# Sending the last 7 MiB of zeros from SyncE's queue in a DMA-bound attention backward kernel

## The chip, the cores and the metric

The kernel runs on one core of one Trainium2 chip. The metric is the time of one execution in device microseconds. The kernel before takes 790.6 us, run after run within about 0.4 us (790.44 to 790.87 us).

Every profile below is of one execution. Its times start at the span's start, and the span ends with the last instruction. PE is TensorE, DVE is VectorE, ACT is ScalarE, POOL is GpSimd, SP is SyncE; a name with a q is that engine's own sequencer, which also issues DMAs.

## The reference, cut to what matters

One decoder block is run forward and backward. Attention reads only the last 4096 of 32768 cache positions, so the gradients of the two caches are zero in all other positions:

```python
W = min(4096, max(256, Sk // 4))           # 4096
k = jnp.repeat(k_cache[:, :, Sk - W:, :], rep, axis=1)
v = jnp.repeat(v_cache[:, :, Sk - W:, :], rep, axis=1)
...
_out, _vjp = jax.vjp(_f, A_x, A_k_cache, A_v_cache, A_wq, A_wo, B_w_gate, B_w_up, B_w_down)
```

The outputs out_2 and out_3 are the gradients of the K and V caches, each of shape (2, 8, 32768, 128) in bfloat16. They hold 224 MiB of zeros and 32 MiB of values. Weights, their gradients and the read part of the caches add some 60 MiB.

## The kernel before

The zeros come from a tile `zt` of 2048 bytes per partition. It is written to DRAM by a casting DMA (bytes in, float32 out), so one row of it makes 8192 bytes of zeros. GpSimd issues these DMAs. There are 32 zero regions of 7 MiB: 29 are issued early, three are cut into 15 pieces that go between the 16 late stores. Four of the early regions are cut unevenly over row counts such as 15 and 12, which gives the 16 DMA engines unequal shares.

```python
ZE = 2048
zt = const.tile([P, ZE], U8)
zero_regions = [o[b, g, 0:Z, :].rearrange("r d -> (r d)") for o in (out_2, out_3) for b in range(B) for g in range(HKV)]
ZPK = Z * DH // 2 // ZE                    # 896 packets of 8192 bytes in a region
ZERO_PARTS = {6: ((4, 1), (15, 2), (2, 2), (15, 14), (12, 2), (P, 4), (16, 7)), 12: ..., 18: ..., 24: ...}
ZERO_FIRST, ZERO_CUTS = 29, (1, 1, 1, 2, 2)
...                                        # zero_cast(i): one region; zero_next(): one late piece
x_bf = load_x(OFF_X)                       # SyncE's queue, 2 KB, the first load
wq_sb = at(OFF_WQ, [P, NDR, HQ * DH], BF16, "wq")
nc.sync.dma_start(out=wq_sb[:], in_=A_wq.rearrange("(p r) n -> p r n", r=NDR))
load_rows(nc.scalar)                       # two loads of 2 KB on ScalarE's queue
...
# the last part: 4 jobs x 2 groups x 2 stores of 2 MiB, from 8 buffers of 16 KB per partition
for a in range(2):
    g0 = gq * 4 + a * 2
    nc.gpsimd.dma_start(out=dst_v[:, b, g0:g0 + 2, :, :], in_=sts[a][:])
    zero_next()
```

The framework gives the DMAs of each issuing path eight completion semaphores (counters that a DMA raises when it has landed) in turn, so each GpSimd DMA waits for the landing of the eighth before it. At the end of the program SyncE waits for all semaphores in a fixed order and then all engines meet at a barrier, a point that none passes before all have reached it.

## Time and profile before

| | before |
|---|---|
| time, median of 4 runs | 790.57 us |
| span of the profiled execution | 788.88 us |
| DMA bytes | 332.44 MB |
| first packet of the first large load (wq) | 2.21 us |
| last DMA packet's end | 786.23 us |
| from that to the span's end | 2.65 us |

The last three rows are read from the trace's records of single DMA packets.

These lines are from the page of the kernel before. Each digit of the DMA line is the busy share of a fortieth of the span (19.7 us) in tenths, and the GB/s line gives what was moved in it. The q0 line is GpSimd's queue, the q1 line SyncE's.

```profile
span 788.9 us, 12410 instructions
...
DMA  8999999999999999999999999999999999999998
GB/s 366 419 417 422 420 426 426 421 430 428 427 422 420 424 425 422 425 425 430 427 428 429 426 430 426 422 430 425 428 428 428 423 429 427 427 428 427 427 429 320
...
q0 software_dynamic: 34576, 268.44, 88.7%
q1 hardware_dynamic: 6932, 63.19, 37.6%
```

The reader is to see a kernel bound by its DMA engines from beginning to end: only the first and last slice are slower. The table of windows of the kernel before says the same of the end. Its columns are the stretch, its length, the busy time of the five engines, TensorE's granted clock, the DMA share and GB/s.

```profile
700.00:740.00 40.00, 19.09 (x56) 6.35 (x57) 20.70 (x32) 16.78 (x29) 5.89 (x9) 0.71 1.07 427
740.00:760.00 20.00, 0.00 (x0) 0.00 (x0) 0.00 (x0) 0.00 (x0) 2.78 (x4) 0.50 1.06 428
```

After 740 us no engine computes, and DMA still moves 428 GB/s. What is left then is queued bytes.

The DMA view of the kernel before over the stretch 755 to 789 us, cut in 40 slices of 0.85 us, shows how the queue runs dry:

```profile
DMA  9999999999999999999999999999989786641000
GB/s 443 434 414 405 463 443 424 424 414 443 424 414 434 434 443 434 414 443 414 443 405 443 414 443 424 424 434 424 386 328 357 328 347 289 279 193 58 0 0 0
```

From about 778 us the rate falls in steps, because the 16 DMA engines do not end together. In the packet records three end about 7 us before the last one, two about 3 us, the rest within 2 us. Averaged over the 16 engines they stand idle for 2.2 us. The three zeros at the end of the line are time with no DMA at all.

Here is what SyncE waited for in the last 29 us of the kernel before (waits that end after 760 us). The columns are the sum, the number of waits and the longest of them.

```profile
SPq L870 <- DMA out_dram<-zt: 164.9, 1, 164.9
SPq L870 <- DMA out_dram<-mem: 14.4, 1, 14.4
SPq L870 <- PEq L870: 1.9, 2, 1.4
```

The middle line is the wait for the last store. The third line is the closing barrier: after everything had landed SyncE still waited 1.4 us for another engine. The profile names TensorE, but TensorE had been idle since before 740 us.

The first issues of SyncE and the first two steps of GpSimd's zeros (start, duration, engine, line, what, and the idle time before) in the kernel before:

```profile
0.81 0.36 SPq L141 DMA_DIRECT2D mem<-in_A_x_dram  x1
1.22 0.37 SPq L145 DMA_DIRECT2D mem<-in_A_wq_dram  x1
```

```profile
13.54 5.37 POOL L315 TENSOR_SCALAR zt<-mem 128x2048 uint8<-128x2048 uint8 x1 [9.84 <-DMA mem<-in_A_wq_dram]
19.22 6.93 POOL L114 DMA_DIRECT2D out_dram<-zt  x8 [0.31 <-POOL zt L315]
```

And GpSimd's last issues before the end:

```profile
745.54 0.71 POOL L844 DMA_DIRECT2D out_dram<-mem  x1 [4.43 <-DMA out_dram<-mem]
747.74 0.68 POOL L130 DMA_DIRECT2D out_dram<-zt  x1 [1.48 <-DMA out_dram<-zt]
752.88 0.71 POOL L844 DMA_DIRECT2D out_dram<-mem  x1 [4.46 <-DMA out_dram<-mem]
```

### The profile page before, as it was taken

To read this page: it belongs to the slowest core of one execution; us is meant where nothing else is said; L and a number is where in the kernel's file an instruction comes from. 1 tells how busy PE (TensorE), PEld (TensorE's weight loads), DVE (VectorE), ACT (ScalarE), POOL (GpSimd) and SP (SyncE) were. 2 spreads that over 40 slices of the span, in tenths; PEclk is the share of its full clock that TensorE was granted. 3 is DMA by queue.
4 is the path that set the end of the run, shared out by engine and by line. 5 is a ranking of instruction groups with operands and counts; after the bars stand their busy time and mean duration, and the time that the engine had idled before them with its cause. 6 is when DMAs were issued, how large, how long until landed. Compare 5 with 4: busy or idle time off the path is not lost. (4 is left out here: it accounts for less than half of the span.)

```text
span 788.9 us, 12410 instructions
## 1 busy us (share of the span) xinstructions
PE 560.2 (71%) x5032; PEld 301.8 (38%) x5096; DVE 474.1 (60%) x1161; ACT 280.7 (36%) x406; POOL 68.9 (9%) x103
## 2 busy tenths in 40 slices
PE   3899998787687989845558779787886675757000
PEld 3656564344565555423225544343332221212000
DVE  2699999126533989854612676755447998757000
ACT  1434330124345334102012426544443674656000
POOL 4300000002000000200000300000100111111100
PEclk9799999867699999987876869855685997788555
DMA  8999999999999999999999999999999999999998
GB/s 366 419 417 422 420 426 426 421 430 428 427 422 420 424 425 422 425 425 430 427 428 429 426 430 426 422 430 425 428 428 428 423 429 427 427 428 427 427 429 320
DMA packets 41578, 332.44 MB, mean 421 GB/s; under 512 B 2592, under 2 KB 2608, under 8 KB 2736
## 3 DMA queue, kind: packets, MB, share of 16 engines
q0 software_dynamic: 34576, 268.44, 88.7%
q1 hardware_dynamic: 6932, 63.19, 37.6%
q8 instruction: 40, 0.66, 0.3%
q10 hardware_dynamic: 12, 0.01, 0.1%
q14 instruction: 18, 0.15, 0.0%
HBM read 49.30 MB, written 282.33 MB: 420 GB/s over the span
## 5 line engine op out<-in xcount | busy, mean ns | idle before, releaser
L422 DVE TENSOR_TENSOR mem<-mem,ee 128x512 bf16<-128x512 bf16 x512 | 181.1, 419 | 26.6 <-PE KT_ps L378 17.4
L433 PE MATMUL M_ps<-mem 128*128 128x512 bf16 x468 | 136.3, 393 | 8.7 <-DVE mem L422 5.3
L836 PE MATMUL ps_g<-mem 128*128 128x512 bf16 x250 | 82.9, 437 | 40.5 <-DVE mem L91 37.7
L91 DVE CAST mem<-ps_g 128x512 bf16<-128x512 f32 x128 | 82.8, 687 | 26.4 <-DMA out_dram<-mem 15.3
L93 ACT CAST mem<-ps_g 128x512 bf16<-128x512 f32 x128 | 74.3, 585 | 50.9 <-PE ps_g L836 44.3
L380 ACT COPY mem<-KT_ps 128x1024 bf16<-128x1024 bf16 x64 | 63.0, 1014 | 69.4 <-PE KT_ps L378 65.5
L114 POOL DMA_DIRECT2D out_dram<-zt x52 | 40.3, 995 | 497.3 <-DMA out_dram<-zt 497.0
L836 PEld LDWEIGHTS <-mem 128*128 128x128 bf16 x256 | 27.5, 108 | 95.3 <-issue 84.3
L254 PE MATMUL ps_tb<-ident_bf,mem 128*128 128x128 bf16 x480 | 56.3, 251 | 9.4 <-DMA mem<-in_B_w_gate_dram 2.8
L433 PEld LDWEIGHTS <-mem 128*128 128x128 bf16 x512 | 43.8, 99 | 48.8 <-issue 15.4
L378 PE MATMUL KT_ps<-ident_bf,mem 128*128 128x128 bf16 x512 | 44.6, 229 | 20.1 <-DMA mem<-in_A_k_cache_dram 16.0
L93 ACT COPY mem<-ps_tb 128x512 bf16<-128x512 bf16 x44 | 25.7, 585 | 72.6 <-PE ps_tb L254 67.8
L254 PEld LDWEIGHTS <-mem 128*128 128x128 bf16 x480 | 37.5, 128 | 35.0 <-issue 30.8
L656 PE MATMUL VT_ps<-ident_bf,mem 128*128 128x128 bf16 x512 | 46.7, 239 | 3.2 <-ACT mem L93 1.1
L656 PEld LDWEIGHTS <-mem 128*128 128x128 bf16 x512 | 36.6, 107 | 27.7 <-issue 20.2
L91 DVE COPY mem<-ps_tb 128x512 bf16<-128x512 bf16 x44 | 18.7, 424 | 42.1 <-PE ps_tb L254 40.7
L665 PE MATMUL dP_ps<-mem 128*128 128x512 bf16 x114 | 40.4, 431 | 4.8 <-ACT mem L93 4.7
L378 PEld LDWEIGHTS <-mem 128*128 128x128 bf16 x512 | 33.6, 102 | 26.6 <-DMA mem<-in_A_k_cache_dram 16.6
L93 ACT COPY mem<-VT_ps 128x1024 bf16<-128x1024 bf16 x31 | 31.7, 1022 | 33.9 <-PE VT_ps L656 32.7
L727 PE MATMUL ps_gr<-mem 2*128 2x512 bf16 (+1 forms) x78 | 33.7, 497 | 12.8 <-DVE mem L747 7.4
L91 DVE CAST mem<-ps_gr 128x512 bf16<-128x512 f32 (+1 forms) x38 | 24.7, 655 | 27.8 <-PE ps_gr L727 27.8
L91 DVE COPY mem<-VT_ps 128x1024 bf16<-128x1024 bf16 x33 | 23.1, 700 | 27.9 <-PE VT_ps L656 27.5
(244 smaller groups left out, 627.1 us busy)
## 6 DMA issues: line engine op xcount, KB each, us to landing
out_dram<-zt POOLq DMA_DIRECT2D x25, 7168.0 KB, 85.5
out_dram<-mem POOLq DMA_DIRECT2D x16, 2048.0 KB, 33.7
mem<-in_A_k_cache_dram SPq DMA_DIRECT2D x16, 1024.0 KB, 21.0
mem<-in_A_v_cache_dram SPq DMA_DIRECT2D x16, 1024.0 KB, 22.0
out_dram<-zt POOLq DMA_DIRECT2D x4, 4096.0 KB, 57.7
out_dram<-zt POOLq DMA_DIRECT2D x6, 2048.0 KB, 32.8
out_dram<-zt POOLq DMA_DIRECT2D x9, 1024.0 KB, 34.0
out_dram<-mem SPq DMA_DIRECT2D x5, 1792.0 KB, 19.0
```

The costliest lines, as they stand in the source:

```text
L91: nc.vector.tensor_copy(out=out, in_=in_)
L93: nc.scalar.copy(out=out, in_=in_)
L114: nc.gpsimd.dma_start(out=dst[done * ZE:(done + rows * n) * ZE].rearrange("(p k e) -> p k e", p=rows, k=n), in_=src.unsqueeze(1).to_broadc ...
L254: nc.tensor.transpose(out=ps[:, a, :], in_=src_block(a), identity=ident_bf[:])
L378: nc.tensor.transpose(out=KT_ps[:, jj, :], in_=Kt[b, g][:, u * 8 + jj, :], identity=ident_bf[:])
L380: nc.scalar.copy(out=KT[:], in_=KT_ps[:])
L422: nc.vector.tensor_tensor(out=pk[:, :, i, :].rearrange("p j (d t) -> p j d t", t=2), in0=Kb[:, j0:j0 + pk_j, :].rearrange("p j (d t) -> p ...
L433: nc.tensor.matmul(out=M_ps[:], lhsT=Vt[b, g][:, j, :], rhs=pk[:, jj, :, :].rearrange("p i d -> p (i d)"), start=(j == 0), stop=(j == NJ - 1))
L656: nc.tensor.transpose(out=VT_ps[:, jj, :], in_=Vt[b, g][:, a * 8 + jj, :], identity=ident_bf[:])
L665: nc.tensor.matmul(out=dP_ps[:, c, :], lhsT=dOpad[:, w0:w0 + P], rhs=VT[:, c * 4:(c + 1) * 4, :].rearrange("d a k -> d (a k)"), start=(i = ...
L727: nc.tensor.matmul(out=ps[:, :n], lhsT=lhsT_fn(k), rhs=rhs_fn(k), start=True, stop=True)
L836: nc.tensor.matmul(out=ps[:, a2, :], lhsT=lhs_bf[:, jp * P:(jp + 1) * P], rhs=rhs_bd[:, ap * 2 + a2, gq * 4:(gq + 1) * 4, :].rearrange("q ...
```

## The change

The change is meant to shorten the end. The zeros are now counted in columns of 1 MiB. Of the 224 columns 205 instead of 203 go early, 12 go between the late stores, and the last 7 leave from SyncE's queue as a plain copy of a zeroed store buffer, with 14336-byte packets. That copy must wait until the last store but one has landed, because it uses its buffer. One column is cut so that eight copies on two rows ("pairs") with small packets stand among the first eight stores. Apart from this, the load of x moves from SyncE's queue to ScalarE's.

```diff
-    ZERO_FIRST, ZERO_CUTS = 29, (1, 1, 1, 2, 2)
...
+    ZCOLS, ZL = ZPK // P, 3584
+    z_cols, PAIR_COL = [0], 216
...
+    def zero_pair(n):
+        nc.gpsimd.dma_start(out=zero_dst(PAIR_COL * P + 112 + 2 * n, 2).rearrange("(p k e) -> p k e", p=2, k=2),
+                            in_=zt[0:P:P // 2, 0:ZE // 2].unsqueeze(1).to_broadcast([2, 2, ZE // 2]))
...
-    x_bf = load_x(OFF_X)
+    x_bf = load_x(OFF_X, nc.scalar)
...
-                for i in range(ZERO_FIRST):
-                    zero_cast(i)
+                zeros(205)
...
+        tail_zeros = list((1, 2, 1, 1, 1, 1, 1, 1, 0, 0, 0, 0, 0, 0, 3, 0))
...
                     nc.gpsimd.dma_start(out=dst_v[:, b, g0:g0 + 2, :, :], in_=sts[a][:])
-                    zero_next()
+                    zeros(tail_zeros.pop(0))
+                    if 0 <= n * 4 + gq * 2 + a < 8:
+                        zero_pair(n * 4 + gq * 2 + a - 0)
...
+        z_last = at(OFF_ST[(st_n[0] - 2) % len(OFF_ST)], [P, 2, ZL // 2], U32, "z_last")
+        nc.vector.memset(z_last[:, 0, :], 0)
+        nc.gpsimd.memset(z_last[:, 1, :], 0)
+        n_last = (len(zero_regions) * ZCOLS - z_cols[0]) * ZE // ZL
+        nc.sync.dma_start(out=zero_dst(z_cols[0] * P, n_last * P * ZL // ZE).bitcast(U32).rearrange("(p k e) -> p k e", p=P, k=n_last),
+                          in_=z_last[:].rearrange("p a e -> p (a e)").unsqueeze(1).to_broadcast([P, n_last, ZL]))
```

More of the change, by code (lines that the diff above doesn't have):

```diff
@@ L107 @@
     ZERO_PARTS = {6: ((4, 1), (15, 2), (2, 2), (15, 14), (12, 2), (P, 4), (16, 7)), 12: ((4, 1), (15, 2), (2, 2), (15, 14), (12, 2), (P, 4), (16, 7)), 18: ((4, 1), (15, 2), (2, 2), (15, 14), (12, 2), (P, 4), (16, 7)), 24: ((3, 16), (15, 2), (3, 4), (15, 18), (12, 2), (P, 4))}
-    ZERO_FIRST, ZERO_CUTS = 29, (1, 1, 1, 2, 2)
-    def zero_cast(i):
-        dst, done = zero_regions[i].bitcast(F32), 0
-        for rows, n in ZERO_PARTS.get(i, ((P, ZPK // P),)):
-            src = zt[0:rows * (P // rows):P // rows, :]
-            nc.gpsimd.dma_start(out=dst[done * ZE:(done + rows * n) * ZE].rearrange("(p k e) -> p k e", p=rows, k=n),
-                                in_=src.unsqueeze(1).to_broadcast([rows, n, ZE]))
-            done += rows * n
-        assert done == ZPK
@@ L119 @@
-    zero_pieces = []
-    for i in range(ZERO_FIRST, len(zero_regions)):
-        done = 0
-        for k in ZERO_CUTS:
-            zero_pieces.append(zero_regions[i].bitcast(F32)[done:done + P * k * ZE].rearrange("(p k e) -> p k e", p=P, k=k))
-            done += P * k * ZE
-        assert done == ZPK * ZE
-    def zero_next():
-        if zero_pieces:
-            dst = zero_pieces.pop(0)
-            nc.gpsimd.dma_start(out=dst, in_=zt[:].unsqueeze(1).to_broadcast([P, dst.shape[1], ZE]))
+    ZCOLS, ZL = ZPK // P, 3584
@@ new lines, with zero_dst, zero_rows @@
+    z_cols, PAIR_COL = [0], 216
+    def zero_dst(pk, n):
+        i, c = divmod(pk, ZPK)
+        assert c + n <= ZPK
+        return zero_regions[i].bitcast(F32)[c * ZE:(c + n) * ZE]
+    def zero_rows(pk, rows, n):
+        src = zt[0:rows * (P // rows):P // rows, :]
+        nc.gpsimd.dma_start(out=zero_dst(pk, rows * n).rearrange("(p k e) -> p k e", p=rows, k=n),
+                            in_=src.unsqueeze(1).to_broadcast([rows, n, ZE]))
+    def zero_pair(n):
+        nc.gpsimd.dma_start(out=zero_dst(PAIR_COL * P + 112 + 2 * n, 2).rearrange("(p k e) -> p k e", p=2, k=2),
+                            in_=zt[0:P:P // 2, 0:ZE // 2].unsqueeze(1).to_broadcast([2, 2, ZE // 2]))
@@ new lines, in zeros @@
+    def zeros(n):
+        while n:
+            i, c = divmod(z_cols[0], ZCOLS)
+            parts = ((16, 7),) if z_cols[0] == PAIR_COL else ZERO_PARTS[i] if c == 0 and n >= ZCOLS and i in ZERO_PARTS else ((P, min(n, ZCOLS - c, PAIR_COL - z_cols[0] if z_cols[0] < PAIR_COL else n)),)
+            done = 0
+            for rows, k in parts:
+                zero_rows(z_cols[0] * P + done, rows, k)
+                done += rows * k
+            z_cols[0] += -(-done // P)
+            n -= -(-done // P)
@@ L137, in load_rows, with load_x @@
         eng.dma_start(out=x_32, in_=A_x.rearrange("b s d -> (b s) d"))
-    def load_x(off):
+    def load_x(off, eng=nc.sync):
         x_bf = at(off, [B, D], BF16, "x")
-        nc.sync.dma_start(out=x_bf[:], in_=A_x.rearrange("b s d -> (b s) d"))
+        eng.dma_start(out=x_bf[:], in_=A_x.rearrange("b s d -> (b s) d"))
         return x_bf
-    x_bf = load_x(OFF_X)
+    x_bf = load_x(OFF_X, nc.scalar)
     wq_sb = at(OFF_WQ, [P, NDR, HQ * DH], BF16, "wq")
```

## The prediction

> **What bounds the kernel now.** The DMA engines. In the page's 40 slices the DMA row reads 9 in all but the first and last, and GB/s stays at 417 to 430 except there (366, 320). DMA moved 332.44 MB. TensorE is 71% busy, VectorE 60%, both idle after 740 us (table of windows). The chain of waits ends in stores. In the late packets an engine starts 8192 bytes every 0.305 us: 16 x 8192 / 0.305 us = 430 GB/s, which makes 774 us of all bytes (estimate), against 790.55. The gap: 2 us before the first load packet, ramp-up, 418 to 425 GB/s where loads and zeros mix, 2.3 us after the last landing, and the uneven end: three of 16 engines finish 6.8 to 7.4 us before the last, the others 0 to 3.7 us. The mean is 2.2 us (estimate), all that an even end could return.
>
> **What the change does.** Bytes stay: 224 MiB of zeros, 32 MiB of cache stores. (1) Two MiB more of zeros go early; the late 21 MiB on GpSimd's queue become 12 there and 7 on SyncE's. (2) Those 7 MiB are a plain copy of a zeroed store buffer, in 14336-byte packets. They wait for the landing of the last store but one and for two memsets, about 1.6 us (estimate, scaled from 0.27 us for 128x256); with issue some 3 us. Behind that store 5 MiB are queued, 12.2 us at 0.409 MiB/us. An engine 7 us ahead still has 2 us of work when SyncE's packets arrive: no gap. (3) Eight pair copies of 16 KB replace part of one column. GpSimd keeps at most eight DMAs outstanding (each waits for the eighth before it), so pairs cut its queue from 14 to 8 MiB, still 19 us of work. If each pair takes the next two engines, every engine keeps its bytes. (4) The load of x moves to ScalarE's queue: wq issues at 0.81 us instead of 1.22.
>
> The Trainium skill (DMA: Bandwidth & Descriptors, "Issuing engines are not separate DMA queues") says that all issuers' DMAs run on the same 16 engines and interleave. This trace agrees: 427 to 430 GB/s whether GpSimd writes alone (690 to 730 us) or SyncE's stores are mixed in (590 to 610). So the queue buys no bandwidth.
>
> **On the critical path.** (4): -0.4 us, since all transfers queue behind the first load. Larger packets (14336 bytes in 0.535 us at best, 8192 in 0.309): -0.1 us. SyncE's mix, 430 instead of 428 for 26 us: -0.1. More DMAs with completion writes: +0.1. A somewhat evener end: -0.5. Sum -1 us.
>
> **Predicted: 789.5 us, 787.6 to 790.7. Chances: faster by over 2% 0.01, within 2% 0.98, slower 0.01.**
>
> **What would show each step.** wq's issue at 0.8 us, the first zeros 0.4 us earlier. Of the last six slices only the last below 420 GB/s. SyncE's last DMA issued near 760 us, landing within 2.5 us of the span's end; the last store landing 5 to 15 us before it. Spread of the engines' last packets still 5 to 9 us. GpSimd's last store issued near 736 instead of 753.
>
> **What would make it wrong.** If the pairs all fall on few engines, or SyncE's packets lighten the late engines, the spread changes and up to 2 us are gained or lost. If compute paces stores 8 to 13, which have no zeros between them, DMA gaps appear near 700 to 735 us and it gets slower.

## The result

The changed kernel takes 789.36 us (median of 4 runs, 789.16 to 789.57) against 790.57 us (790.53 to 790.62). The ratio is 0.9985, with a 95% interval of 0.9967 to 1.0002: the same at the 2% limit, and 1.2 us less in the medians. (A ratio is the mean time of one kernel's fast runs over that of the other's fast runs of the same rounds, so it is not quite the ratio of the medians.) All four runs of the change are below all four of before, but the interval includes 1, so the size of the gain rests on the traces and on the runs below as well.

The page of the kernel after:

```profile
span 787.5 us, 12487 instructions
...
DMA  9999999999999999999999999999999999999998
GB/s 374 418 418 422 418 426 426 422 429 427 428 419 420 426 424 424 424 424 432 426 430 426 427 428 428 422 429 426 428 425 429 421 431 425 428 426 427 427 432 344
...
q0 software_dynamic: 33984, 261.10, 86.4%
q1 hardware_dynamic: 7456, 70.53, 40.5%
```

The 7 MiB have moved from q0 to q1, and the rates of the 38 middle slices are the same to within 3 GB/s. The windows of the kernel after have no gap in the DMA either, although no zeros stand between stores 8 and 13:

```profile
700.00:740.00 40.00, 22.65 (x68) 7.32 (x66) 23.20 (x36) 20.16 (x35) 8.81 (x13) 0.82 1.04 427
740.00:760.00 20.00, 0.00 (x0) 0.00 (x0) 1.55 (x1) 0.00 (x0) 1.60 (x1) 0.50 1.04 428
```

The DMA view of the kernel after over the same stretch, 755 to 789 us:

```profile
DMA  9999999999999999999999999999887877620000
GB/s 405 424 453 443 453 357 453 458 434 400 426 451 484 412 429 422 446 436 410 434 424 439 422 439 439 422 439 388 371 354 337 354 304 320 270 118 0 0 0 0
```

The staircase of the ending engines is the same as before, one slice earlier. The SyncE waits that end after 770 us, for the kernel after:

```profile
SPq L882 <- DMA out_dram<-mem: 26.1, 2, 14.4
SPq L882 <- PEq L882: 0.7, 2, 0.5
```

The longest barrier wait is 0.5 us where it was 1.4 us. At the start:

```profile
0.81 0.39 SPq L149 DMA_DIRECT2D mem<-in_A_wq_dram  x1
```

```profile
13.14 5.37 POOL L319 TENSOR_SCALAR zt<-mem 128x2048 uint8<-128x2048 uint8 x1 [9.43 <-DMA mem<-in_A_wq_dram]
18.82 6.93 POOL L118 DMA_DIRECT2D out_dram<-zt  x8 [0.31 <-POOL zt L319]
```

The first large load, and with it the first zeros, are 0.4 us earlier. At the end GpSimd and SyncE issue:

```profile
733.39 0.86 POOL L848 DMA_DIRECT2D out_dram<-mem  x1
757.29 1.60 POOL L856 MEMSET mem<- 128x1792 uint32 x1 [23.04 <-issue]
```

```profile
759.38 0.65 SPq L858 DMA_DIRECT2D out_dram<-mem  x1
```

The packet records split the span of the two profiled executions into three parts:

| us | before | after | difference |
|---|---|---|---|
| span's start to wq's first packet | 2.21 | 1.84 | -0.37 |
| that to the last packet's end | 784.02 | 783.95 | -0.07 |
| last packet's end to span's end | 2.65 | 1.66 | -0.99 |
| span | 788.88 | 787.45 | -1.43 |

So the transfers take as long as before. The gain lies in front of them and, most of it, behind them.

The trace's records of the single instructions show what happens behind. At the end of its program each engine executes a DRAIN. GpSimd's DRAIN does not end before its own DMAs are finished. In the kernel before GpSimd's last packet ends at 786.23 us, its DRAIN at 788.09 us, 1.87 us later, and the span ends 0.78 us after the DRAIN. SyncE had checked all semaphores and reached the barrier at 786.88 us, so it waited for GpSimd. In the kernel after GpSimd's last packet ends at 774.09 us and its DRAIN at 776.13 us, while SyncE's zeros are still moving. The last packet of all is SyncE's, at 785.79 us, SyncE reaches the barrier at 786.69 us, and nobody is left to wait for. All 14 traces agree: the long DRAIN ends 1.64 to 2.27 us after the last packet of GpSimd's queue, in ten of them while SyncE's bytes still move for some 10 us. So it follows GpSimd's own queue and not the end of all transfers.

My theory was then: (1) the earlier first load gives some 0.4 us, (2) having SyncE's queue end last takes GpSimd's DRAIN off the end and gives 1.0 us, (3) nothing else counts. The rivals were that the use of SyncE's queue as such moves bytes faster or evens out the engines, and that the pairs do something.

### The profile page after: what moved, and what is told of

Same layout as the page of the kernel before. It is cut to its first block, busy times and chain, and to the rows that moved or that the text cites. A ratio compares the mean times of both kernels' runs of the same rounds, so it can differ in the third digit from the quotient of the medians.

```text
span 787.5 us, 12487 instructions
## 1 busy us (share of the span) xinstructions
PE 568.4 (72%) x5096; PEld 303.8 (39%) x5096; DVE 475.0 (60%) x1162; ACT 280.9 (36%) x406; POOL 72.7 (9%) x108
## 5 line engine op out<-in xcount | busy, mean ns | idle before, releaser
L436 PE MATMUL M_ps<-mem 128*128 128x512 bf16 x512 | 140.2, 392 | 6.5 <-DVE mem L425 6.1
L840 PE MATMUL ps_g<-mem 128*128 128x512 bf16 x256 | 84.6, 442 | 39.8 <-DVE mem L91 36.9
L118 POOL DMA_DIRECT2D out_dram<-zt x63 | 47.0, 941 | 501.4 <-DMA out_dram<-zt 500.7
L381 PE MATMUL KT_ps<-ident_bf,mem 128*128 128x128 bf16 x512 | 46.6, 236 | 24.7 <-DMA mem<-in_A_k_cache_dram 19.7
L668 PE MATMUL dP_ps<-mem 128*128 128x512 bf16 x128 | 44.3, 434 | 4.2 <-ACT mem L93 4.2
L381 PEld LDWEIGHTS <-mem 128*128 128x128 bf16 x512 | 35.2, 106 | 30.5 <-DMA mem<-in_A_k_cache_dram 20.3
```

Source lines behind the costliest of these rows:

```text
L118: nc.gpsimd.dma_start(out=zero_dst(pk, rows * n).rearrange("(p k e) -> p k e", p=rows, k=n), in_=src.unsqueeze(1).to_broadcast([rows, n, ZE]))
L381: nc.tensor.transpose(out=KT_ps[:, jj, :], in_=Kt[b, g][:, u * 8 + jj, :], identity=ident_bf[:])
L436: nc.tensor.matmul(out=M_ps[:], lhsT=Vt[b, g][:, j, :], rhs=pk[:, jj, :, :].rearrange("p i d -> p (i d)"), start=(j == 0), stop=(j == NJ - 1))
L668: nc.tensor.matmul(out=dP_ps[:, c, :], lhsT=dOpad[:, w0:w0 + P], rhs=VT[:, c * 4:(c + 1) * 4, :].rearrange("d a k -> d (a k)"), start=(i = ...
L840: nc.tensor.matmul(out=ps[:, a2, :], lhsT=lhs_bf[:, jp * P:(jp + 1) * P], rhs=rhs_bd[:, ap * 2 + a2, gq * 4:(gq + 1) * 4, :].rearrange("q ...
```

## The experiments

"Stretch" is the time from wq's first packet to the last packet, "rest" the time from there to the span's end, both in the profiled run. The kernel before, run on the same chip in the same rounds, was at 790.59 or 790.60 us. All results were correct.

| run | edit | median us | stretch | rest |
|---|---|---|---|---|
| before | | 790.57 | 784.02 | 2.65 |
| after | | 789.36 | 783.95 | 1.66 |
| e1 | before, x on ScalarE's queue | 790.37 | 784.11 | 2.62 |
| e12 | before, tail on SyncE only | 789.60 | 783.97 | 1.65 |
| e2 | after, tail on GpSimd | 790.62 | 784.30 | 2.91 |
| e3 | after, SyncE sends 3 MiB, GpSimd ends last | 791.05 | 784.43 | 3.04 |
| e4 | after, no pairs | 789.27 | 784.11 | 1.66 |
| e7 | after, 8192-byte packets | 789.59 | 784.32 | 1.67 |
| e5 | after, probe copies | 789.38 | 784.18 | 1.67 |
| e8 | after, zeros cut evenly | 801.90 | 796.57 | 1.64 |
| e10 | after, one region less cut unevenly | 791.16 | 785.96 | 1.66 |
| e6 | after, last semaphore by cut K loads | 790.03 | 785.25 | 1.25 |
| e9 | after, last semaphore by small loads | 789.00 | 784.23 | 1.23 |
| e11 | e4, e9 and e10 together | 790.52 | 785.16 | 1.24 |

### e1: only the load of x

```diff
-    x_bf = load_x(OFF_X)
+    x_bf = load_x(OFF_X, nc.scalar)
```

> The kernel before with one edit: x is loaded by ScalarE's queue. Theory (the first load goes out earlier, nothing else changes): wq issued at 0.81 us instead of 1.22, first zeros 0.4 us earlier, time 0.3 to 0.5 us less than before (about 790.15), end after the last packet unchanged at about 2.65 us. Rival (the whole gain of the change comes from the end): 790.55.

Measured: 790.37 us against 790.60, so 0.23 us less. The first packet of wq is at 1.79 us, 0.42 us earlier, and the rest is 2.62 us as before; the stretch is 0.09 us longer. The first step of the zeros starts at 13.30 us instead of 13.54, only 0.24 us earlier, where the expectation said 0.4. That is the size of the gain in time. The part is smaller than I thought. The interval of the ratio (0.9985 to 1.0010) includes 1, and the slowest runs of e1 (790.50) touch the fastest of before (790.48), so the time alone does not prove it; the earlier packets in the trace do show it.

### e12: only the tail

```diff
 (the change, without zero_pair and its column, and with)
-    x_bf = load_x(OFF_X, nc.scalar)
+    x_bf = load_x(OFF_X)
```

> The kernel before with the late zeros as in the change and the last 7 MiB on SyncE's queue, but no pairs and x still on SyncE's queue. Theory (drain): stretch after the last packet 1.66 us instead of 2.65, time 0.9 to 1.1 us less than before, 789.6; with the earlier first load (0.23 us measured alone) it makes up the whole change. Rival (the parts do not add up): outside 789.3 to 789.9.

Measured: 789.60 us, 0.99 us less than before (ratio 0.9987, 0.9975 to 1.0000). The rest is 1.65 us instead of 2.65 and the stretch is as before. SyncE's waits in e12 that end after 760 us:

```profile
SPq L880 <- DMA out_dram<-mem: 26.2, 1, 26.2
SPq L880 <- PEq L880: 0.6, 2, 0.5
```

The long barrier wait is gone, as in the kernel after. With e1's 0.23 us this makes 1.22 us; the whole change makes 1.21 us. To within the scatter of the runs the two parts add up, and nothing is left for the pairs to explain.

### e2: the tail on GpSimd's queue

```diff
-        z_last = ...
-        nc.vector.memset(z_last[:, 0, :], 0)
-        nc.gpsimd.memset(z_last[:, 1, :], 0)
-        nc.sync.dma_start(...)
+        zeros(len(zero_regions) * ZCOLS - z_cols[0])
```

> The kernel after, but the last 7 MiB leave from GpSimd's queue behind the last store, no memset, no SyncE copy. Drain theory (the gain at the end is that GpSimd's closing DRAIN no longer ends last): stretch from last packet to the end of the span 2.6 us instead of 1.66, time about 1.0 us more than after, 790.3. Rival (SyncE's larger packets or the mix of two queues move bytes faster, or even out the engines): first wq packet to last packet gets longer than 783.95 us by 0.5 us or more, and the stretch after it stays at 1.7 us.

Measured: 790.62 us, 1.26 us more than after. The waits of SyncE that end after 780 us show the long barrier wait again:

```profile
SPq L877 <- DMA out_dram<-zt: 163.0, 1, 163.0
SPq L877 <- PEq L877: 1.8, 2, 1.3
```

The rest is 2.91 us; GpSimd's DRAIN ends 2.13 us after the queue's last packet. The stretch is 0.35 us longer than after's, less than the 0.5 us that I had set for the rival, but not nothing.

### e3: both queues at the end, GpSimd's last

```diff
-    ZCOLS, ZL = ZPK // P, 3584
+    ZCOLS, ZL = ZPK // P, 2048
-        tail_zeros = list((1, 2, 1, 1, 1, 1, 1, 1, 0, 0, 0, 0, 0, 0, 3, 0))
+        tail_zeros = list((1, 2, 1, 1, 1, 1, 1, 1, 0, 0, 0, 0, 0, 0, 3, 4))
```

> The kernel after, but SyncE sends only the last 3 MiB and GpSimd 4 MiB more behind the last store, so both queues are used at the end and GpSimd's lands last. Drain theory: stretch after the last packet 2.6 us, time as with the tail on GpSimd, 790.3, although SyncE still sends zeros. Rival (use of SyncE's queue as such gives the gain): about 789.4 to 789.8. (Its packets are 8192 bytes, needed for the size.)

This run tells the theory from the rival best, because SyncE's queue is used and only the order of landing differs. Measured: 791.05 us. SyncE's waits in it:

```profile
SPq L882 <- DMA out_dram<-zt: 27.3, 1, 27.3
SPq L882 <- PEq L882: 1.8, 2, 1.3
```

SyncE's last packet of zeros ends at 780.16 us, GpSimd's last packet at 786.25 us, so the order of landing is the intended one. The rest is 3.04 us and the DRAIN ends 2.27 us after the last packet. Using SyncE's queue gives nothing; ending with it gives the gain. The run is 0.75 us slower than the 790.3 us of the drain theory. Some 0.4 us of this is in the rest, 3.04 us instead of 2.6, because the DRAIN took longer to end; the stretch is 0.5 us longer than after's, and why was not tried.

### e4: no pairs

```diff
-    z_cols, PAIR_COL = [0], 216
+    z_cols, PAIR_COL = [0], 10 ** 6
-                    if 0 <= n * 4 + gq * 2 + a < 8:
-                        zero_pair(n * 4 + gq * 2 + a - 0)
```

> The kernel after without the eight pair copies (the column goes as an ordinary 1 MiB copy). Theory (the pairs move no bytes between engines and do not pace anything on the critical path): 789.2 to 789.5, finish spread of the engines 6.8 to 7.3 us as after. Rival (the shorter GpSimd queue that the pairs make is part of the gain): 789.8 or more, with a slower or more uneven end.

Measured: 789.27 us, ratio to before 0.9983 against 0.9985 for the change. The engines' ends spread over 7.3 us (7.1 after). The pairs can be left out. They do make GpSimd's queue shorter, but it is long enough either way.

### e7: smaller packets

```diff
-    ZCOLS, ZL = ZPK // P, 3584
+    ZCOLS, ZL = ZPK // P, 2048
```

> The kernel after with SyncE's 7 MiB in 8192-byte packets instead of 14336. My prediction credited the larger packets with 0.1 us: then 789.4 to 789.5 and first-to-last stretch about 784.05. If packets of 8192 bytes cost SyncE's queue more, as in the 3 MiB run (784.43, time 791.05), then 789.7 or more with a stretch of 784.3 or more.

Measured: 789.59 us, 0.2 us more than after, between what I set for the two cases; the two ratios to before, 0.9986 and 0.9985, lie well within each other's intervals. The stretch of the one profiled run, 784.32 us, lies just in what I had set for the costlier case, but e4 and e5 with large packets have 784.11 and 784.18 us. The packet size is worth some 0.2 us or nothing and is not settled closer.

### e5 and e8: which engines end early, and why

Three engines end 7 us early in every run, so a better split could return up to 2 us. e5 puts copies on 15 rows and on 2 rows, with packets of a size that nothing else has, into the stretch where only GpSimd's queue runs, and e8 takes the uneven cuts away.

```diff
 (e5)
+    probe = [(15, 1)] + [(2, 2)] * 8 + [(15, 1), (2, 1)]      # rows, packets of 2048 bytes per row
 (e8)
-    ZERO_PARTS = {6: ..., 12: ..., 18: ..., 24: ...}
+    ZERO_PARTS = {}
```

> The kernel after with the eight pairs replaced by a probe: one copy on 15 rows, eight pairs, one copy on 15 rows, one on 2. It is for the trace. Theory (a copy of k rows takes the next k engines in turn): the pairs start one engine earlier than in the kernel after, so that the three engines that finish 7 us early show in other pairs, alone or two together; with both runs each of the three is told from its neighbour. Rival (a pair always takes the same two engines): all pairs would show the same lead over the last engine. Time as after, 789.4 within 0.5.

Measured: in the kernel after the two packet groups of the fourth, fifth and eighth pair start 6.3 to 6.7 us apart, those of the other pairs at most 2.0 us. In the probe it is the same three pairs, with 6.3, 6.8 and 6.9 us. So the rival is out, since the pairs differ, but my rule is out too: the copy on 15 rows did not shift the pairs. The three early engines sit in three different pairs. Both copies on 15 rows show only two packets with a lead of 7 us over their last, so the engine that they leave out seemed to be the third early one.

> The kernel after with the zero regions cut evenly over the 16 engines (no odd row counts). It shows what the uneven cuts are worth and which engines are slow by themselves. If one engine is slow and the cuts give it about 50 packets of 0.305 us less, it now finishes up to 15 us after the others: time 795 to 805 us. Rival (the cuts no longer matter): 789 to 790.

Measured: 801.90 us, 12.5 us more. In the DMA view of e8 from 762 to 800 us (0.95 us per slice) the end looks like this:

```profile
DMA  9999999410009998999969999899960000000000
GB/s 414 440 414 440 423 431 397 181 60 26 26 34 479 479 463 343 403 476 485 431 295 492 476 476 386 356 468 483 483 257 15 30 30 30 30 15 30 30 0 0
```

One engine falls behind. Near 771 us 15 engines have emptied their queue and one still works, at 26 GB/s: it holds back the landing of the last store but one, and SyncE's zeros must wait for that. From 790 us it ends alone again, 7.8 us after the others. The uneven cuts spare this engine, and they are worth ten times the whole change.

The engine is not slow at the end: alone, from 790.9 us on, it takes 0.535 us for each packet of 14336 bytes, as long as the fastest ones in the kernel after. It falls behind bit by bit. Between 365 and 493 us, in the stretches of e8 without loads, the last completion of a 7 MiB region (read as this engine's each time) follows the one before after 17.5 to 17.9 us, the first completion after 17.0 to 17.1 us. Why, no run shows. Packets of program instructions could land on one engine and take its time, but the one region without any such packet still took 17.5 us, so they are at most a part.

### e10: one region less cut unevenly

```diff
-    ZERO_PARTS = {6: ..., 12: ..., 18: ((4, 1), (15, 2), ...), 24: ...}
+    ZERO_PARTS = {6: ..., 12: ..., 24: ...}
```

> The kernel after with one of the four unevenly cut zero regions cut evenly. In the probe both copies on 15 rows left out an engine that finishes 7 us early. Theory (the cuts relieve that engine, by more than it needs): one engine gets 16 packets of 0.305 us = 4.9 us more, its lead falls from 7 to about 2 us, only two engines still end 7 us early, the other 15 end 0.3 us earlier: 789.0 to 789.1. Rival (the relieved engine is one of those that end last, the early ones are early by themselves): time 3 to 5 us more.

Measured: 791.16 us, 1.8 us more than after. In the packet records three engines still end 7.9 us before the last, or 5.8 to 5.9 us before the others, and one engine now ends 2.0 us after all others. So my reading of the probe falls: the engine that the cuts relieve is not one of the three early ones. The size of the loss lies between the two that I had set. Which engines the three are, and how to give them more, stays open.

### e6 and e9: the order of the semaphores

After the last landing SyncE checks the remaining semaphores one after the other, 0.06 us each. In the kernel after its last copy has the first of the eight semaphores of that path. Seven more DMAs ahead of it give it the last one.

```diff
 (e6)
+        if b == 1 and g < 7:
+            for a in range(2):
+                nc.sync.dma_start(out=Kt[b, g][:, a * NJH:(a + 1) * NJH, :], in_=Kv[:, b, g, a * NJH:(a + 1) * NJH, :])
 (e9, ahead of z_last)
+        for i in range(7):
+            nc.sync.dma_start(out=x_bf[:, i * 32:(i + 1) * 32], in_=A_x.rearrange("b s d -> (b s) d")[:, i * 32:(i + 1) * 32])
```

> The kernel after, with seven loads of K of the second batch split in halves, so that SyncE's last copy gets the last of its eight completion semaphores instead of the first. At the end SyncE then checks about one semaphore after the landing instead of eight, each 0.06 us. Theory: stretch after the last packet 1.2 to 1.3 us instead of 1.66, time 0.4 us less than after, 788.95. Rival (the checks overlap something else): as after.

Measured: the rest is 1.25 us as expected, but the stretch is 1.3 us longer and the time 790.03 us. The row of e6 in its table of windows, 200 to 300 us, and that of the kernel after:

```profile
200.00:300.00 100.00, 87.50 (x1051) 56.79 (x1051) 61.95 (x181) 40.84 (x48) 3.00 (x5) 0.88 1.26 420
```

```profile
200.00:300.00 100.00, 87.94 (x1063) 56.37 (x1061) 59.00 (x171) 39.90 (x45) 3.19 (x6) 0.92 1.40 423
```

3 GB/s over 100 us are 0.3 MB, or 0.7 us at 427 GB/s: about half of the loss, if the rounded rates are taken as they are. It is the largest difference of eight such stretches. That the halved loads cause it was not tried further.

> The kernel after with seven loads of 64 elements each (into a buffer that is dead by then) ahead of SyncE's last copy, so that it gets the last of the eight completion semaphores without cutting the K loads, whose cutting lengthened the DMA stream by 1.3 us in the run before. Theory: first-to-last stretch as after, 783.95 to 784.2, stretch after the last packet 1.25 us, time 788.9 to 789.1. If the time is as after (789.3 to 789.5), the checks are not worth removing or the small loads cost as much.

Measured: 789.00 us (788.89 to 789.08), ratio to before 0.9979 (0.9967 to 0.9992); the rest is 1.23 us; the stretch, 784.23 us, is just above what I had expected. SyncE's last issues in e9:

```profile
607.46 17.73 SPq L855 DMA_DIRECT2D mem<-in_A_x_dram  x7
759.64 0.63 SPq L860 DMA_DIRECT2D out_dram<-mem  x1
```

The seven small loads lie in a time when SyncE has nothing else to issue. This version is 1.6 us faster than before and 0.4 us faster than the change. It is the fastest, by the seven useless loads of 128 bytes each.

### e11: three small things together

```diff
 (e4, e9 and e10 together)
```

> The kernel after without pairs, with the seven small loads and with one region cut evenly. If the three small effects add up: 788.4 to 788.8, faster than before by about 1.9 us and than after by 0.7 us.

Measured: 790.52 us. e10's loss is in it; the rest of 1.24 us shows that e9's gain is too. It should have been run without the cut of e10.

## Why the prediction was right

The time, 789.36 us, is 0.14 us from the predicted 789.5 and inside the range. But two terms of the sum were wrong and cancelled: 0.6 us were credited to the stretch, which gave 0.07, and nothing to the end behind the last packet, which gave 1.0. That the number came so close was luck.

- **The bound** was right: DMA at 417 to 432 GB/s in all middle slices, in both kernels.
- **The earlier first load**, predicted -0.4 us: wq is issued at 0.81 us instead of 1.22 as stated, the first zeros are 0.4 us earlier. Alone it is worth 0.23 us (e1), where the zeros came only 0.24 us earlier.
- **No gap**: right. SyncE's copy was issued at 759.38 us (I said near 760), GpSimd's last store at 733.4 (736), the last store's last packet ended 11.7 us before the end of SyncE's copy (5 to 15), and of the last six slices only the last is under 420 GB/s. The two memsets took 1.55 and 1.60 us, as estimated.
- **"Larger packets ... -0.1 us", "SyncE's mix ... -0.1", "More DMAs ... +0.1", "A somewhat evener end: -0.5"**: the sum of these is -0.6 us in the stretch from first to last packet, and that stretch changed by 0.07 us. The mis-sized term is the evener end: the mean idle time of the engines went from 2.2 to 2.0 us, and the ends spread over 7.1 us, within the 5 to 9 that I stated myself. I had written that every engine keeps its bytes; then nothing could make the end evener, and crediting it with 0.5 us had no ground. "SyncE's mix" rested on a wrong reading as well: I took 590 to 610 us for a stretch with SyncE's stores mixed in, but SyncE moved 0.44 of 8.5 MB there. From 610 to 630 us, where it moved 3.76 of 8.45 MB, the rate was 423 GB/s, against 428 with GpSimd alone (690 to 730).
- **"2.3 us after the last landing"**: I named this time in the gap and treated it as fixed. It is the step that failed, and it is the largest part of the gain: 1.0 us (e12), because GpSimd's DRAIN ends about 2 us after its queue's last packet, and SyncE is through 0.9 us after its own. With GpSimd's queue landing last the rest is long again, 2.91 us in e2 and 3.04 us in e3.
- **"So the queue buys no bandwidth"** was right, though not by the evidence that I gave: e3 uses both queues at the end and its stretch is 0.4 us longer than that of the kernel before, and from 762 to 769 us the kernel after moves 425 GB/s with both queues where the kernel before moves 430 with one.
- **The pairs** do nothing measurable (e4). My rule that "each pair takes the next two engines" fits in so far as the pairs' leads differ; the probe did not follow the rule for 15 rows.

## What to carry to other kernels

When a kernel ends in a DMA, look behind the last packet: which engine's program ends last, and what its last instruction waits for. Here it paid to let the last bytes leave from SyncE's queue while GpSimd's closing DRAIN ran in its shadow, and to give that last DMA the semaphore that is checked last. And where one DMA engine falls behind the others, the cut of the bytes over them can be worth far more than the order of the queues (12.5 us against 1.2 here), so measure it first.

## What the Trainium skill lacked or had wrong

- GPSIMD Engine Reference: the page does not say that the DRAIN at the end of GpSimd's program waits for the DMAs that it issued. In the four runs in which GpSimd's queue ended last (before, e1, e2, e3) it ended 1.85 to 2.27 us after the queue's last packet, and the program's end followed 0.77 to 0.78 us later. In the ten others it ended 1.64 to 2.19 us after that packet.
- VectorE: DVE Perf Modes, "The DRAIN you can't avoid", calls the DRAINs of a program's beginning and end a constant of about 12 ns on all engines. SyncE's are 7 ns here, but the first of GpSimd's three closing ones is recorded with 35.2 us in the kernel before, since it waits, and the first closing ones of TensorE, ScalarE and VectorE with 0.60 to 0.73 us.
- DMA: Bandwidth & Descriptors, "Anatomy of one DMA", puts most of a fixed cost of about 2 us on the receipt of the last write, ahead of the semaphore. In the kernel before, GpSimd's last packet of data starts at 785.91 us and SyncE has seen the semaphore at 786.59 us, 0.68 us later, so no 2 us lie ahead of the semaphore. A delay of about 2 us shows only in GpSimd's DRAIN; whether it is the same cost, no run tells.
- The same page, "Latency and other measured facts", says that engines 7 and 15 are usually slower. With equal shares one engine fell behind here: it ended 7.8 us after the rest, which had stood idle for some 3 to 5 us before (e8). With the unequal shares three others end 7 us before the last. Which numbers they all have, no run shows.
- The same page, "Queues, rings and completion order", says that a semaphore's write lands only after every earlier write from that DMA engine, across its queues. A consequence that it does not draw shows in e3: SyncE's last packet of zeros ended at 780.16 us, but 13 of the 16 semaphore writes of that copy ended 4.9 to 5.8 us after they had begun, together with GpSimd's, the last at 786.25 us. A queue that is done can so be reported done only with the other queue.
